# Two products of batch 0 by a second Strassen level, the softmax behind a later sum, and four small sums on GpSimd

## The chip, the cores and the metric

The kernel runs on one core of one Trainium2 chip. The metric is the device time of one execution in microseconds. The engines' names are those of the profile: PE is TensorE, DVE VectorE, ACT ScalarE, POOL GpSimd, and SP the queue that issues the transfers.

## The reference: what is computed

A cross attention between a sequence and a small state, and then a feed-forward layer over both results. All data is fp32.

```python
B, H, S, Ns, D = 8, 8, 512, 32, 64
scores = scale * x @ state^T                  # (B, H, S, Ns)
a = exp(scores - max); a /= a.sum(-1) + 1e-9
xread = a @ state                             # (B, H, S, D)
a2 = softmax of scale * state @ x^T           # the same scores, turned
sread = a2 @ x                                # (B, H, Ns, D)
x = concat(xread, sread) as 8 * 544 = 4352 rows of 512
h = x @ w_in                                  # 512 x 2048
g = where(h > 0, h, exp(min(h, 0)) - 1)
out = g @ w_out                               # 2048 x 512
```

The inputs are x (8, 8, 512, 64), state (8, 8, 32, 64), w_in (512, 2048) and w_out (2048, 512); the output has 4352 rows of 512.

## The kernel before

**Order.** No loop in the kernel runs as written. Every operation is recorded with a cost in a `Plan`; a list scheduler then brings all of them into one order, and each engine gets its instructions in that order. TensorE's operations are taken in the program's order as soon as they can start, the other engines' by a due time reckoned back from TensorE's; GpSimd's are kept in the order in which the program records them (L288), and transfers go through one queue, SP. `plan.behind(op)` (L189) makes all operations recorded under it, but those of GpSimd, wait for `op`. The profile puts all recorded operations at L466, the line of the helper that emits them, so they are told apart by their tiles.

**Batches.** The work goes batch by batch, 512 rows each. Batches 0 and 1 are computed together in `start()`, which also converts the weights into fp32 tiles and makes sums of them. Then come the rest of batch 1 (`ffn2_1`), batches 2 to 7 (`batch`, with `ffn2` as its second half), and the 256 rows of sread (`states`).

**The first layer of a batch.** The attention's weights are folded into the layer: `make_m` and `make_three` multiply the state with w_in (tile w_half, fetched from a DRAM copy, tile kT for the state) into tile m, and the softmaxed scores in aT are then multiplied with m. `ffn1_chunk` does this for a quarter of the 2048 columns by Strassen-Winograd with seven products: `sum_a` (L743) makes three sums of aT's blocks once per batch and `sum_m` four of m's for each quarter. `sum_a` runs on VectorE, `sum_m` on GpSimd. ELU goes through tile xe into tile g; batch 0's activations lie in `sec[:, :8192]` (called g0), all others' in g.

**Between two batches.** While the second layer of batch b runs on TensorE, `soft_next` (L1423) prepares batch b+1: `softmax` turns the scores by VectorE transposes into xr, takes maxima, subtracts them on GpSimd, takes exp on ScalarE, multiplies with the reciprocals on GpSimd, and transposes into aT; `softmax_rows` does the softmax along the other direction; `load_x` loads x into xe; `move_state` (L829) transposes xr and moves it by 16 transfers xr to xr; then `sum_a` and the first `sum_m`. All of it stands behind `late[3]`, the last of the sums of the second layer's product 4. `state_read` (L842) multiplies the moved xr with xe; ELU may overwrite xe only after it.

**The second layer.** g times w_out is a first level of Strassen-Winograd (class `Strassen`), seven products P1 to P7 of 256x256-blocks. A plain product (L1095) is 16 times two matmuls of 128x128 by 128x256 into one PSUM bank, and its result is then copied by ScalarE (`copy`) or added by VectorE (`plus`) into quarters of the output tile. In `ffn2` and `ffn2_1` most products go by a second level (class `Second`, L973): four sums of weights of 128x512 (`weights`, kept for all batches), three or four sums of activations (`sums`), and seven steps of four matmuls of 128x128 each (`steps`) in two banks x and y; after every step VectorE adds the bank into the output, and the next step in the same bank waits for it. The weights' sums of P7, P5, P4, P3 and P6 have homes of 1536 columns each in sec; `s_2` in sec holds two pairs of activation sums.

**Batch 0.** In `start()` batch 0's seven products are plain ones (object n0). In the order of the program: P1, P2, P6 (t_w[2]), P7 (t_w[3]), the scores of batch 2, P5 (t_w[1]), P4 (t_w[4]) and P3 (b22). `n1.sum_1()` between P5 and P4 makes batch 1's first sums. The weights' sums of 6, 7, 5, 4, 3 and 2 are all made in `ffn2_1`.

**Fetches.** Each batch fetches the halves 0 to 7 of w_in into three places of w_half, where half hc goes to place hc modulo 3; halves 5, 6 and 7 are recorded at the start of `batch` (L1523) for `make_three(b, (6, 7), 5)`.

Of the kernel before, what the change touches and what calls it, by code (L numbers as in the profile page):

```python
# [391 lines left out]
def kernel(  # L392
# [350 lines left out]
    def sum_a():  # L743

        r11, r12, r21, r22 = a_blocks_of(a_sb)
        t1, t2, t4 = (a_sb[:, 1024 + 256 * i : 1280 + 256 * i] for i in range(3))
        (V if 1 else Q).tensor_tensor(out=t1, in0=r12, in1=r11, op=ALU.subtract)
        (V if 1 else Q).tensor_tensor(out=t2, in0=r22, in1=t1, op=ALU.subtract)
        (V if 1 else Q).tensor_tensor(out=r12, in0=r22, in1=r12, op=ALU.subtract)
        (V if 1 else Q).tensor_tensor(out=t4, in0=r21, in1=t2, op=ALU.subtract)  # L750
# [168 lines left out]
    def ffn1_chunk(b, c, g_to):  # L919

        m = g_of[b, c]
        l11, l12, s3, l22 = m_blocks(m)
        s1, s2, s4 = (m[:, 1024 + 256 * i : 1280 + 256 * i] for i in range(3))
        r11, t3, r21, r22 = a_blocks_of(a_sb)
        t1, t2, t4 = (a_sb[:, 1024 + 256 * i : 1280 + 256 * i] for i in range(3))
        pa, pc, pb = bank(), bank(), fixed[c % 2].view()
        u2, u3 = (
            sec[:, 7680 + (c % 2 * 2 + i) * 512 : 7680 + (c % 2 * 2 + i + 1) * 512] for i in range(2)
        )
# [24 lines left out]
        return part_1, part_2  # L954
# [18 lines left out]
    class Second:  # L973

        def __init__(self, t, spare=None):
            self.t = t.rearrange("p (i k q) -> p i k q", i=3, q=P)
            self.spare = spare

        def blocks(self, b):
# [80 lines left out]
                steps.append(lambda args=args: step(*args))  # L1060
            return steps

    second = {
        k: Second(sec[:, i * 1536 : (i + 1) * 1536]) for i, k in enumerate((7, 5, 4, 3, 6))
    }
    second[2], second[1] = Second(sec_2), Second(sec_1)

    def spaces(ap, n=2):
        return [ap[:, i * 512 : (i + 1) * 512] for i in range(n)]

    s_2 = [spaces(sec[:, 7680 + i * 1024 : 7680 + (i + 1) * 1024]) for i in range(2)]

    class Strassen:

# [78 lines left out]
        for i in range(3)  # L1153
    ]

    def weight_block(n, parts=1):

        out = []
        for i in range(parts):
# [12 lines left out]
        return out  # L1172
# [16 lines left out]
    def start():  # L1189
# [23 lines left out]
        for what in 'swxtvyu':  # L1213
            if what == "s": load_states(0, 1, raw_s, q2)
            if what == "x": load_x(0, x_halves, q2)
            if what == "w": blocks[0] = weight_block(0, 2)
# [93 lines left out]
        y = o.open()  # L1310
        o.product(y, o.a21, t_w[3], True)
        o.copy(y, 1, 1)
        scores(2, xr, [f.view() for f in fixed] if 1 else None)
        softmax(2, a_sb)
        softmax_rows(2)
        load_x(2, x_halves)
        o.product(x1, o.s, t_w[1], False)
        o.plus(x1, 1, 1)
        n1.sum_1()
        o.product(y, o.a22, t_w[4], False)  # L1320
        o.plus(y, 1, 0)
        o.product(x1, o.a12, b22, False)
        o.copy(x1, 0, 1)
        for i in (1, 0):
            store(0, i, o)
        return n1, held[1]
# [30 lines left out]

    def ffn2(o, b):

        c11, c12, c21, c22 = (o.part(i, j) for i in range(2) for j in range(2))  # L1360
        nxt = b + 1 < B
        spare = spaces(m_sb[:, 1], 3)
        sl = 0
        if not sl: o.sum_1()
        late = [plan.ops[-1]]
        if 0:
# [55 lines left out]

        def soft_next():  # L1423
            if nxt:
                with plan.behind(late[3]):
                    softmax(b + 1, a_sb)
                    softmax_rows(b + 1)
                    load_x(b + 1, x_halves)
                    move_state(b + 1)
                    sum_a()  # L1430
                    if 1:
                        sum_m(m_to[0])
# [18 lines left out]
        for f in steps:  # L1451
            f()
        store(b, 0, o)

    def ffn2_1(o, b, x1):

# [30 lines left out]
        next_m(b + 1)  # L1487
# [34 lines left out]
    def batch(b):  # L1522
        for hc in range(5, 8) if 1 else range(4, 7):  # L1523
            fetch(hc)
        if b + 1 < B:
            load_blocks(b + 1, ob)
        else:
            make_ident()
# [105 lines left out]
    def states():  # L1634
# [7 lines left out]
        for hc in range(5):  # L1642
            fetch_state(hc)
        for k, i in second.items():
            if k > 1 or 0: i.restore()
# [102 lines left out]
```

## Time and profile before

| What | us |
|---|---|
| median of 4 runs | 696.54 |
| the runs | 695.88, 696.77, 696.47, 696.61 |
| the profiled execution's own time (the first of them) | 695.88 |
| its span, first to last instruction | 694.0 |
| TensorE busy (granted clock 1.000) | 684.4 |
| VectorE busy | 572.5 |
| ScalarE busy | 302.1 |
| GpSimd busy | 112.7 |

The span is 1.88 us shorter than the time; that part lies around the profiled instructions. A group or a timeline line gives engine, line, operation, the tile written and the tiles read, the shape and the number of instructions; in a timeline the first two numbers are the start and the length in us, and brackets give the idle time before and what ended it. A matmul of fp32 shows as two records, so x32 in a plain product is 16 matmuls, and x8 in a second-level step is four. Matmuls are pipelined, so their lengths overlap; the distance of two starts is the time that one takes.

### The profile page before, as it was taken

Reading aid. Unit: us, or ns where it says so; the run is one execution under the profiler, and the core shown is the slowest. Engines: PE = TensorE matmul, PEld = TensorE weight load, DVE = VectorE, ACT = ScalarE, POOL = GpSimd, SP = SyncE. Lnnn points to the kernel's source line nnn. Section 1 sums busy time; section 2 is a strip of 40 time slices with the busy share of each in tenths; the row PEclk is TensorE's granted clock in tenths of the full one; section 3 lists DMA queues with packets and bytes.
Section 4 is the critical chain, followed back from the end, with each engine's and each line's share of the span. In section 5 each row is a group of like instructions: output and inputs, shape, how many; then the busy total and the mean of one; then the engine's idle time right before and its main releaser. Section 6 shows DMA issues by size and latency. Waiting matters only on the chain.

```text
span 694.0 us, 14567 instructions
## 1 busy us (share of the span) xinstructions
PE 684.4 (99%) x5782; PEld 590.4 (85%) x5782; DVE 572.5 (82%) x1019; ACT 302.1 (44%) x640; POOL 112.7 (16%) x133
## 2 busy tenths in 40 slices
PE   8899999999999999999999999999999999999997
PEld 7444478889988998889988998899888998899996
DVE  5999999879949994999679985999499966997640
ACT  4999971003157313722275215731373227500530
POOL 0100000003330151104230243015110423000000
PEclk9999999999999999999999999999999999999999
DMA  9867873202281507450562218150745043200300
GB/s 234 259 203 253 278 240 51 61 31 92 80 218 38 122 20 231 87 122 4 177 156 81 44 47 243 46 123 19 240 78 123 2 150 126 61 1 32 122 8 24
DMA packets 111268, 78.55 MB, mean 113 GB/s; under 512 B 89184, under 2 KB 92768, under 8 KB 111200
## 3 DMA queue, kind: packets, MB, share of 16 engines
q1 hardware_dynamic: 108988, 77.06, 40.0%
q8 instruction: 46, 0.75, 0.5%
q10 hardware_dynamic: 2212, 0.56, 0.4%
q14 instruction: 22, 0.18, 0.1%
HBM read 61.34 MB, written 13.11 MB: 107 GB/s over the span
## 4 chain that ended last, share of the span: by engine, by line
PE 91%; ACT 3%; DMA 2%; SPq 1%; DVE 1%; issue 0%; ACTq 0%
PE ps L466 91%; SPq L466 1%; ACT sec L466 1%; DMA g<-in_x_dram 1%; DMA w_half<-w_in_mem 1%; ACT t_w L466 0%; DVE w_half L466 0%; ACT o L466 0%; DVE sec L466 0%; ACT w_half L466 0%; ACT m L466 0%; ACT g L466 0%; ACT s L466 0%; DVE t_w L466 0%; DVE g L466 0%
## 5 line engine op out<-in xcount | busy, mean ns | idle before, releaser
L466 PE MATMUL ps<-aT,m 128*128 128x256 f32 (+1 forms) x568 | 147.9, 405 | 0.1
L466 PE MATMUL ps<-w_out,g 128*128 128x128 f32 (+1 forms) x864 | 144.2, 314 | 0.0
L466 PEld LDWEIGHTS ps<-w_out,g 128*128 128x128 f32 x864 | 126.3, 191 | 12.4 <-issue 4.2
L466 PEld LDWEIGHTS ps<-aT,m 128*128 128x128 f32 x568 | 106.2, 190 | 29.4 <-issue 14.5
L466 DVE TENSOR_TENSOR o<-o,ps 128x128 f32<-128x128 f32 (+2 forms) x239 | 66.2, 281 | 41.3 <-PE ps L466 40.5
L466 ACT COPY o<-ps 128x128 f32<-128x128 f32 (+2 forms) x70 | 23.1, 335 | 147.4 <-PE ps L466 141.4
L466 POOL TENSOR_TENSOR xr<-xr,small 128x512 f32<-128x512 f32 x24 | 30.0, 1271 | 334.9 <-DVE small L466 171.1
L466 PE MATMUL ps<-sec 128*128 128x128 f32 x560 | 74.8, 277 | 0.0
L466 PEld LDWEIGHTS ps<-sec 128*128 128x128 f32 x560 | 68.5, 192 | 4.0 <-DVE o L466 3.7
L466 POOL TENSOR_TENSOR m<-m 128x256 f32<-128x256 f32 x72 | 60.5, 860 | 27.1 <-ACT m L466 25.7
L466 PE MATMUL ps<-t_w,s 128*128 128x128 f32 (+1 forms) x432 | 64.5, 298 | 0.0
L466 ACT ACTIVATE xe<-ps 128x512 f32<-128x512 f32 x96 | 54.9, 601 | 19.4 <-PE ps L466 12.8
L466 PEld LDWEIGHTS ps<-t_w,s 128*128 128x128 f32 x432 | 58.6, 192 | 2.5
L466 ACT COPY m<-ps 128x512 f32<-128x512 f32 (+1 forms) x56 | 28.1, 540 | 62.1 <-PE ps L466 55.7
L466 DVE SCALAR_TENSOR_TENSOR g<-xe,ps 128x512 f32<-128x512 f32 x66 | 43.7, 679 | 9.8 <-ACT xe L466 6.2
L466 DVE TENSOR_TENSOR ps<-sec,ps 128x512 f32<-128x512 f32 (+1 forms) x52 | 34.8, 669 | 13.9 <-ACT sec L466 7.0
L466 ACT COPY sec<-ps 128x512 f32<-128x512 f32 (+1 forms) x52 | 29.7, 571 | 28.6 <-PE ps L466 28.5
L466 PE MATMUL ps<-aT,s 128*128 128x256 f32 x168 | 41.2, 379 | 0.0
L466 ACT ACTIVATE xe<-xe 128x512 f32<-128x512 f32 x66 | 39.8, 636 | 0.7
L466 PEld LDWEIGHTS ps<-aT,s 128*128 128x128 f32 x168 | 31.9, 190 | 4.3
L466 PE MATMUL ps<-w_half,kT 64*32 64x256 f32 x1024 | 34.9, 381 | 0.5 <-DVE g L466 0.3
L466 PE MATMUL ps<-sec,g 128*128 128x128 f32 (+1 forms) x252 | 31.5, 272 | 1.2 <-DMA g<-in_x_dram 1.2
(149 smaller groups left out, 1108.6 us busy)
## 6 DMA issues: line engine op xcount, KB each, us to landing
w_half<-w_in_mem SPq DMA_DIRECT2D x54, 512.0 KB
t_w<-in_moe_w_out_dram SPq DMA_DIRECT2D x8, 1024.0 KB
t_w<-in_moe_w_in_dram SPq DMA_DIRECT2D x7, 1024.0 KB
out_dram<-o SPq DMA_DIRECT2D x14, 512.0 KB
xe<-in_x_dram SPq DMA_DIRECT2D x26, 256.0 KB
o<-in_x_dram SPq DMA_DIRECT2D x80, 64.0 KB
w_in_mem<-w_half SPq DMA_DIRECT2D x8, 512.0 KB
xr<-xr SPq DMA_DIRECT2D x96, 32.0 KB
```

The source lines that it names most:

```text
L466: ins = getattr(engine, name)(**named)
```

## The change

It does three things.

1. Batch 0's P4 and P3 go by the second level. For that, the weights' sums of 4 and 3 are made in `start()` and no longer in `ffn2_1`. The homes of the weights' sums of 4, 3, 7 and 5 and of `s_2` are rows of batch 0's own activations in sec (two by two, even rows for 4 and 3, odd rows for 7 and 5), and those of 6 stay behind them. P7's add into quarter (1, 0) is recorded right after P7, and P5's bank is copied into quarter (0, 1) right after its add into quarter (1, 1), because P4's and P3's steps are added to these quarters. The eight weights' sums of 4 and 3 and the activations' sums of both products run on VectorE in the time of batch 0.
2. What `soft_next` records stands behind `late[6]`, the last sum of activations of product 7, in place of `late[3]`, that of product 4; the sums of 6 and of 7 lie between.
3. `sum_a`'s four subtractions per batch go from VectorE to GpSimd.

TensorE's operations of `ffn2` also get the last `make_m` as something to wait for in the plan. Toggles that are off change nothing.

The program has 24 matmuls more on TensorE (56 in the place of 32), 24 operations more on GpSimd, two fewer on VectorE and as many as before on ScalarE and in the queue SP. In its order, the fetches of halves 5, 6 and 7 stand ahead of move_state's 16 transfers; before they stood behind them.

```diff
 def sum_a():
-        (V if 1 else Q).tensor_tensor(out=t1, in0=r12, in1=r11, op=ALU.subtract)
+        (V if 0 else Q).tensor_tensor(out=t1, in0=r12, in1=r11, op=ALU.subtract)
...
-    second = {
-        k: Second(sec[:, i * 1536 : (i + 1) * 1536]) for i, k in enumerate((7, 5, 4, 3, 6))
-    }
...
-    s_2 = [spaces(sec[:, 7680 + i * 1024 : 7680 + (i + 1) * 1024]) for i in range(2)]
+    if 1:
+        rows = sec[:, :8192].rearrange("p (r e c) -> p r e c", e=2, c=512)
+        homes = {
+            4: rows[:, 0:3, 0], 3: rows[:, 3:6, 0], 7: rows[:, 0:3, 1], 5: rows[:, 3:6, 1],
+            6: sec[:, 8192:9728],
+        }
+        second = {k: Second(homes[k]) for k in (7, 5, 4, 3, 6)}
+        s_2 = [[rows[:, 6, i], rows[:, 7, i]] for i in range(2)]
...
 in start():
         o.product(y, o.a21, t_w[3], True)
         o.copy(y, 1, 1)
+        if 1:
+            o.plus(y, 1, 0)
         scores(2, xr, [f.view() for f in fixed] if 1 else None)
         softmax(2, a_sb)
         softmax_rows(2)
         load_x(2, x_halves)
         o.product(x1, o.s, t_w[1], False)
         o.plus(x1, 1, 1)
-        n1.sum_1()
-        o.product(y, o.a22, t_w[4], False)
-        o.plus(y, 1, 0)
-        o.product(x1, o.a12, b22, False)
-        o.copy(x1, 0, 1)
+        if 1:
+            o.copy(x1, 0, 1)
+        if 1 < 2: n1.sum_1()
+        if 1:
+            second[4].weights(t_w[4])
+            second[4].sums(o.a22, s_2[0] + [sec_2[:, 1024:]])
+            steps = second[4].steps(o.part(1, 0))
+            second[3].weights(b22)
+            for f in steps:
+                f()
+            second[3].sums(o.a12, spaces(sec_2))
+            for f in second[3].steps(o.part(0, 1)):
+                f()
...
 in ffn2():
+        made = [op for op in plan.ops if op.name == "make_m"][-1]
+        first_op = len(plan.ops)
...
-                with plan.behind(late[3]):
+                with plan.behind(late[6]):
                     softmax(b + 1, a_sb)
                     softmax_rows(b + 1)
                     load_x(b + 1, x_halves)
                     move_state(b + 1)
                     sum_a()
...
+        for op in plan.ops[first_op:]:
+            if op.engine == PE and 1:
+                op.deps.add(made)
...
 in ffn2_1():
-        second[4].weights(t_w[4])
+        if not 1: second[4].weights(t_w[4])
...
-        second[3].weights(b22)
+        if not 1: second[3].weights(b22)
```

More of the change, by code (lines that the diff above doesn't have):

```diff
@@ L746, in sum_a @@
         t1, t2, t4 = (a_sb[:, 1024 + 256 * i : 1280 + 256 * i] for i in range(3))
-        (V if 1 else Q).tensor_tensor(out=t1, in0=r12, in1=r11, op=ALU.subtract)
-        (V if 1 else Q).tensor_tensor(out=t2, in0=r22, in1=t1, op=ALU.subtract)
-        (V if 1 else Q).tensor_tensor(out=r12, in0=r22, in1=r12, op=ALU.subtract)
-        (V if 1 else Q).tensor_tensor(out=t4, in0=r21, in1=t2, op=ALU.subtract)
+        (V if 0 else Q).tensor_tensor(out=t1, in0=r12, in1=r11, op=ALU.subtract)
+        (V if 0 else Q).tensor_tensor(out=t2, in0=r22, in1=t1, op=ALU.subtract)
+        (V if 0 else Q).tensor_tensor(out=r12, in0=r22, in1=r12, op=ALU.subtract)
+        (V if 0 else Q).tensor_tensor(out=t4, in0=r21, in1=t2, op=ALU.subtract)
     def a_blocks_of(a):
@@ L926, in ffn1_chunk @@
         pa, pc, pb = bank(), bank(), fixed[c % 2].view()
-        u2, u3 = (
-            sec[:, 7680 + (c % 2 * 2 + i) * 512 : 7680 + (c % 2 * 2 + i + 1) * 512] for i in range(2)
-        )
+        u2, u3 = s_2[c % 2]
         e = [xe[:, i * 512 : (i + 1) * 512] for i in range(4)]
@@ L975, in __init__ @@
         def __init__(self, t, spare=None):
-            self.t = t.rearrange("p (i k q) -> p i k q", i=3, q=P)
+            if len(t.shape) == 2:
+                t = t.rearrange("p (i c) -> p i c", i=3)
+            self.t = t.rearrange("p i (k q) -> p i k q", q=P)
             self.spare = spare
@@ L1061, in steps @@
             return steps
-    second = {
-        k: Second(sec[:, i * 1536 : (i + 1) * 1536]) for i, k in enumerate((7, 5, 4, 3, 6))
-    }
-    second[2], second[1] = Second(sec_2), Second(sec_1)
     def spaces(ap, n=2):
         return [ap[:, i * 512 : (i + 1) * 512] for i in range(n)]
-    s_2 = [spaces(sec[:, 7680 + i * 1024 : 7680 + (i + 1) * 1024]) for i in range(2)]
+    if 1:
[6 more added lines that the diff above has]
+        s_2 = [[rows[:, 6, i], rows[:, 7, i]] for i in range(2)]
+    else:
+        second = {
+            k: Second(sec[:, i * 1536 : (i + 1) * 1536]) for i, k in enumerate((7, 5, 4, 3, 6))
+        }
+        s_2 = [spaces(sec[:, 7680 + i * 1024 : 7680 + (i + 1) * 1024]) for i in range(2)]
+    second[2], second[1] = Second(sec_2), Second(sec_1)
     class Strassen:
@@ L1154, with weight_block @@
     ]
-    def weight_block(n, parts=1):
+    def weight_block(n, parts=1, only=None):
         out = []
-        for i in range(parts):
+        for i in range(parts) if only is None else (only,):
             k = 4 // parts
@@ L1215, in start @@
             if what == "x": load_x(0, x_halves, q2)
-            if what == "w": blocks[0] = weight_block(0, 2)
+            if what == "w": blocks[0] = weight_block(0, 2, 0 if "W" in 'swxtvyu' else None)
+            if what == "W": blocks[0] += weight_block(0, 2, 1)
             if what == "t": load_states(1, 2, raw_s[:, 1:], (SP,))
@@ L1318, in start @@
         o.plus(x1, 1, 1)
-        n1.sum_1()
-        o.product(y, o.a22, t_w[4], False)
-        o.plus(y, 1, 0)
-        o.product(x1, o.a12, b22, False)
-        o.copy(x1, 0, 1)
+        if 1:
[11 more added lines that the diff above has]
+                f()
+        else:
+            o.product(y, o.a22, t_w[4], False)
+            o.plus(y, 1, 0)
+            o.product(x1, o.a12, b22, False)
+            o.copy(x1, 0, 1)
+        if 1 == 2: n1.sum_1()
         for i in (1, 0):
@@ L1365, in ffn2 @@
         late = [plan.ops[-1]]
-        if 0:
+        if 0 or b in []:
             second[1].sums(o.a11, spare + s_2[0][:1])
@@ L1524, in batch @@
             fetch(hc)
+        if b in [][:1]: second[1].weights(b11)
         if b + 1 < B:
@@ L1644, in states @@
         for k, i in second.items():
-            if k > 1 or 0: i.restore()
+            if k > 1 or 0 or []: i.restore()
         xT = st["xT"].rearrange("p m b s -> p m (b s)")
```

## The prediction

> **What bounds the kernel now.** I read the page's first part and its chain, then the pieces of the chain in order of time, then the timelines of TensorE and VectorE around batch 0's products, and last all engines around one steady boundary between batches (300 to 350 us).
>
> The page: busy time, chain by engine, two GpSimd groups.
>
> ```profile
> PE 684.4 (99%) x5782; PEld 590.4 (85%) x5782; DVE 572.5 (82%) x1019; ACT 302.1 (44%) x640; POOL 112.7 (16%) x133
> PE 91%; ACT 3%; DMA 2%; SPq 1%; DVE 1%; issue 0%; ACTq 0%
> L466 POOL TENSOR_TENSOR xr<-xr,small 128x512 f32<-128x512 f32 x24 | 30.0, 1271 | 334.9 <-DVE small L466 171.1
> L466 POOL TENSOR_TENSOR m<-m 128x256 f32<-128x256 f32 x72 | 60.5, 860 | 27.1 <-ACT m L466 25.7
> ```
>
> The chain in order of time (start, us, what), its end.
>
> ```profile
> 62.20 427.89 PE ps L466 x3561
> 490.09 7.42 DMA w_half<-w_in_mem
> 497.51 0.04 issue
> 497.55 191.77 PE ps L466 x1536
> ```
>
> TensorE is the bound from 62.20 on: one chain without a gap, but for the third fetch of a weight half at 497.55. So a matmul saved after 62 us is time saved, and a wait of TensorE is time lost; what the other engines do counts only where TensorE stands behind it.
>
> TensorE (start, length), batch 0's products and four later second-level steps.
>
> ```profile
> 135.03 7.07 PE L466 MATMUL ps<-t_w,s 128*128 128x256 f32 x32
> 141.94 7.07 PE L466 MATMUL ps<-t_w,sec 128*128 128x256 f32 x32
> 148.85 7.07 PE L466 MATMUL ps<-w_out,sec 128*128 128x256 f32 x32
> 155.75 1.95 PE L466 MATMUL ps<-t_w,s 128*128 128x128 f32 x16
> ...
> 166.22 1.06 PE L466 MATMUL ps<-t_w,s 128*128 128x128 f32 x8
> ...
> 169.80 0.39 PE L466 MATMUL ps<-sec,g 128*128 128x128 f32 x2
> ```
>
> The starts are what to read: P5 at 135.03, P4 at 141.94, P3 at 148.85, the next work at 155.75. P4 and P3 last 6.91 and 6.90 us. Four steps of four matmuls run from 166.22 to 169.80, 0.895 us each.
>
> VectorE in the same place.
>
> ```profile
> 130.42 1.17 DVE L466 TENSOR_TENSOR s<-s,sec 128x1024 f32<-128x1024 f32 x1
> 131.52 0.67 DVE L466 TENSOR_TENSOR sec<-w_out 128x512 f32<-128x512 f32 x1
> ...
> 138.69 1.23 DVE L466 TENSOR_TENSOR s<-g 128x1024 f32<-128x1024 f32 x1 [2.76 <-PE ps L466]
> ```
>
> It has no pause up to 135.9, and then waits 2.76 us for TensorE. A 512-wide sum starts 0.60 us after the one before it, a 1024-wide one 1.13, a 128x128 add 0.20.
>
> The steady boundary.
>
> ```profile
> 313.56 2.05 POOL L466 TENSOR_TENSOR xr<-xr,small 128x512 f32<-128x512 f32 x2 [32.98 <-PE ps L466]
> 322.11 3.04 POOL L466 TENSOR_TENSOR xr<-xr,small 128x512 f32<-128x512 f32 x2 [6.50 <-DVE small L466]
> 322.41 1.82 DVE L466 TENSOR_TENSOR s<-s,g 128x1024 f32<-128x1024 f32 x1
> 327.85 10.07 SPq L466 DMA_DIRECT2D xr<-xr  x16
> 337.05 1.89 PE L466 MATMUL ps<-aT,m 128*128 128x256 f32 x8
> 341.55 1.10 PE L466 MATMUL ps<-xe,xr 128*32 128x64 f32 x64
> ```
>
> **The change, part by part.**
>
> (a) *TensorE's work.* P4 and P3 were 13.81 us. They become 14 steps: 14 x 0.895 = 12.53. Term: -1.28 us.
>
> (b) *What the steps wait for.* The weights' sums of 4 and 3 (eight 512-wide sums) and both products' activation sums move onto VectorE at batch 0, where it was already full up to 135.9. In the built program its queue runs as before up to the second s<-s,sec (three sums in, four out, so 0.60 earlier: ends 130.9). Then 11 sums of 0.60: 137.5. P7's add, 0.60: 138.1. Four more sums: 140.5. Then in order s<-g (1.13), a sum (0.60), g<-g,s (1.13), P5's add into quarter (1,1) (0.60), s<-g (1.13), the add of P4's step 0 (0.20), g<-g,s (1.13), the add of step 1 (0.20). Their ends: 141.7, 142.3, 143.4, 144.0, 145.1, 145.35, 146.5, 146.7.
> On TensorE, P5 ends at 141.94, steps 0 and 1 at 143.73, and then the scores of batch 2 stand. They alternate between two banks, and one of them held P5. That bank is first added by VectorE (144.0) and then copied by ScalarE into quarter (0,1); the built program makes the copy wait for the add. With 0.4 for the copy (the mean of ScalarE's copies into o is 335 ns) and two handovers of about 0.15 (VectorE's idle between a matmul's end and its add at 322.20), the scores get the bank at about 144.75 instead of 143.73, a stall of 1.0 us. Step 2 wants step 0's add (145.35) and finds it done; step 3 wants step 1's add (146.7) and starts about 0.2 us late. Behind step 3 I followed the queue to 161 us and found no further wait above 0.1. Term: +1.2 us. Bounds: 0 (VectorE some 1.3 us further than I reckon) and +1.3 (all of the lateness of step 1's add). I take 1.2, since the queue is told by rows of this very place.
> What hides the remaining VectorE work (eight sums, 4.8 us, twelve net adds of 0.2) is that batch 1's steps lose the same eight sums; they ran without a wait of TensorE before, so that gain is nothing.
>
> (c) *The third fetch.* Before, fetches 5, 6, 7 are issued at 338.02, behind the 16 transfers of move_state, and the matmuls that need them start at 346.30; at the one boundary of the chain they landed 7.42 us after issue and TensorE stood some 0.4 us. In the new SP order they stand ahead of move_state, right behind the matmuls that free their slots (which end at 330.7), so some 15 us before their use. Term: -0.4, between 0 and -0.8 (twice the one seen).
>
> (d) *The softmax, two sums later.* Its transposes xr<-ps now wait for the sums of 7, in the profile the g<-g sum that ends at 317.97; with 3.7 us of softmax work out of its way (two transposes at 0.63, four reductions at 0.60) that sum ends by some 314.9 and the transposes start near 315.5, against 308.21. From there to the first aT transpose was 16.1 us; I take 17.3 to 18.5, since the reductions now lie between more adds. So aT is ready at 332.8 and 334.4. Behind it:
> - GpSimd: the four sums of aT at 0.84 each (the 3.35 of four m<-m at 325.10), 334 to 337.1, then the m<-m to 340.4. POOL keeps program order, so these m<-m wait behind them. TensorE's first aT pair in the new order needs none of the sums; five steps lie behind it, and the sums are first needed about 342.3. Slack 2 to 4 us. VectorE loses four sums of 0.33 to 0.42.
> - SP: move_state issues from about 335.85 (xr<-xr transposes 8 us later than 326.41) for 10.07 us (11.98 at the longest of the boundaries), last packets 1.0 us behind the last issue: 346.9 to 348.8. The transfers now share the queue with the three fetches. State_read in the new order stands behind 14 aT matmuls (0.43 each), five steps and make_three (1.45): 337.05 + 11.97 = 349.0. Slack 0.2 to 2.1 us. Behind state_read stand all matmuls of the next batch, and ELU, which overwrites xe.
> - VectorE beside GpSimd: the pair of GpSimd operations took 2.05 alone and 3.04 where s<-s,g ran, and that took 1.82 instead of 1.22; under m<-m at 331.58 the 512-wide sums took 0.84, 0.87 and 1.21 instead of 0.68. Four new GpSimd sums per batch meet VectorE sums before P3's steps, whose adds (due about 337.9) stand behind them: 0 to 0.2 us per boundary.
> GpSimd's sums of aT come at six boundaries (batches 2 to 7), the later softmax at five (3 to 7). Term for all: +0.3. Lower end 0: TensorE has no wait here that could go. Upper end +4, if state_read comes 0.8 late at each of five.
>
> A rule that speaks against this part: the Trainium skill's "SBUF — State Buffer", section "Who interferes with whom", says that a VectorE instruction with two SBUF inputs and a GpSimd one that reads SBUF exclude each other for the whole instruction. Read so, each of 24 sums could hold VectorE for its full 0.84, and if one in two fell ahead of an add that TensorE wants, the sum would be 10 us worse (an estimate). The rows above show 0.16 to 0.6 of lengthening per sum, not a full block, and adds that read PSUM stay at 0.28 to 0.29 under the same GpSimd work; I go by the rows.
>
> Sum against the profiled execution (span 694.0, its time 695.88, the lowest of four): 695.88 - 1.28 + 1.2 - 0.4 + 0.3 = 695.7. The median, 696.54, lies 0.66 above it, for reasons no view shows; a change that takes a fetch's lateness away may take some of that too. I predict 695.8.
>
> **The rivals.**
> - *VectorE is in time* (faster). P4's stall in (b) is 0: 695.88 - 1.28 - 0.4 + 0.2 = 694.4. For it: VectorE idles 2.76 us before 138.69 today and my lateness is only about 1 us, a sixth of what I summed. Against: the bank of P5 goes through two engines before the scores.
> - *State_read comes late* (slower). move_state's last transfers land behind 349.0. At 0.6 us for each of five boundaries: 695.7 - 0.3 + 3.0 = 698.4. It decides from a softmax about 1 us later than I reckon, or transfers that take over 12 us behind the fetches; above 0.5 us per boundary the kernel is slower in measure (695.7 - 0.3 + 2.5 = 697.9). For it: the slack is the smallest of all here, and every piece of the chain before it crosses three engines. Against: 1 us of middle slack.
> - *The fetches stay late* (no part of (c) comes): 696.1, inside the forecast.
>
> **How the numbers follow.** 0.2% of 696.54 is 1.39 us, about what a measurement can tell from no change: faster is below 695.15, slower above 697.93. The forecast (part of the gain eaten, 695.2 to 697.0) has 0.43, with the late fetches in it; VectorE in time 0.32; state_read late 0.25. Faster 0.33, same 0.43, slower 0.24, as little of each case spills over. The range goes from 694.3 (the faster case, less its last tenth) to 698.6 (state_read 0.64 late).
>
> **What would show it.** (a) 14 steps 0.895 us apart where P4 and P3 were. (b) A gap of about 1 us before or within the scores near 144, with VectorE's add of P5 at 143.4 to 144; right if it is there, wrong if the steps run on. (c) No DMA piece near 497 in the chain. (d) POOL's aT sums ending by 338, state_read near 349 with no gap before it; a gap there, five times, is the slower rival. I am wrong altogether if TensorE shows new waits in batch 1's steps or between aT matmuls.

## The result and the profile after

The changed kernel is 2 us slower.

| | before | after |
|---|---|---|
| median, us | 696.72 (71 runs) | 698.71 (44 runs) |
| lowest and highest, us | 695.35, 700.26 | 696.28, 701.95 |
| ratio, 95% interval | | 1.0026 (1.0019 to 1.0033) |
| profiled execution: its time, its span, us | 695.88, 694.0 | 697.24, 695.4 |

Two numbers have to be explained, and they are not the same: the two profiled executions differ by 1.36 us, the medians by 1.99. The forecast was 695.8, with a range up to 698.6.

The page of the changed kernel, busy time by engine; and the end of the chain of waits (start, length, what).

```profile
PE 686.0 (99%) x5830; PEld 591.2 (85%) x5830; DVE 564.7 (81%) x1017; ACT 302.7 (44%) x640; POOL 123.1 (18%) x157
```

```profile
62.75 121.52 PE ps L466 x817
184.27 0.03 issue
184.30 166.16 PE ps L466 x1522
350.46 0.06 issue
350.52 340.21 PE ps L466 x2926
```

The chain still runs on TensorE alone from 62 us on, and the piece that waited for the third fetch is gone. But such a chain hides short waits inside its pieces; they show only where the distance of two starts is longer than the work. Laying the two traces side by side, from the start of the TensorE-bound stretch (62.20, now 62.75) to its end (689.32, now 690.73) the difference of 1.41 us falls into three parts:

- +0.55 before that stretch begins. This is start-up (loads and weight conversion); in the other profiles of this study the stretch begins anywhere from 62.0 to 63.6, but for one whose start was put in another order (67.39).
- -0.02 from P5 to the scores of batch 3 (135.03 to 226.04 before, 135.58 to 226.57 after). The second level's 1.28 us are gone again by then.
- +0.88 at the five steady boundaries. Their periods were 75.21, 75.21, 75.21, 75.62 (0.41 of it the fetch) and 74.32, and are 75.45, 75.60, 75.42, 75.42 and 74.56.

TensorE around batch 0's scores, after (start, length).

```profile
141.63 1.03 PE L466 MATMUL ps<-t_w,s 128*128 128x256 f32 x4
142.49 1.95 PE L466 MATMUL ps<-t_w,sec 128*128 128x128 f32 x16
144.37 1.86 PE L466 MATMUL ps<-xr,kT 64*32 64x512 f32 x16
146.16 1.16 PE L466 MATMUL ps<-sec 128*128 128x128 f32 x8
```

VectorE in the same place.

```profile
140.92 1.21 DVE L466 TENSOR_TENSOR s<-g 128x1024 f32<-128x1024 f32 x1
142.06 0.68 DVE L466 TENSOR_TENSOR sec<-t_w,sec 128x512 f32<-128x512 f32 x1
142.66 1.21 DVE L466 TENSOR_TENSOR g<-g,s 128x1024 f32<-128x1024 f32 x1
143.79 0.68 DVE L466 TENSOR_TENSOR m<-m,ps 128x512 f32<-128x512 f32 x1
```

The scores (the row with 64x512) take 1.79 us from their start to the next step; undisturbed they take 1.02. So TensorE waits 0.77 us there, and about 0.2 more behind it. The last VectorE row is the add of P5's bank that the scores stand behind; it starts at 143.79, and VectorE has no pause ahead of it from 117 us on. In the profile of before VectorE stood idle 2.76 (ahead of 138.69), 0.44, 0.30 and 2.76 us in this stretch:

```profile
142.21 0.69 DVE L466 TENSOR_TENSOR m<-m,ps 128x512 f32<-128x512 f32 x1 [0.44 <-PE ps L466]
145.59 0.69 DVE L466 TENSOR_TENSOR t_w<-t_w 128x512 f32<-128x512 f32 x1 [0.30 <-PE ps L466]
149.05 0.69 DVE L466 TENSOR_TENSOR m<-m,ps 128x512 f32<-128x512 f32 x1 [2.76 <-PE ps L466]
```

One steady boundary after: GpSimd, the transfer queue and TensorE.

```profile
332.43 2.05 POOL L466 TENSOR_TENSOR xr<-xr,small 128x512 f32<-128x512 f32 x2 [10.26 <-DVE small L466]
334.45 0.72 POOL L466 TENSOR_TENSOR aT<-aT 128x256 f32<-128x256 f32 x1
335.56 2.10 POOL L466 TENSOR_TENSOR aT<-aT 128x256 f32<-128x256 f32 x3 [0.39 <-DVE aT L466]
```

```profile
331.67 1.29 SPq L466 DMA_DIRECT2D w_half<-w_in_mem  x3
336.83 10.08 SPq L466 DMA_DIRECT2D xr<-xr  x16
```

```profile
347.36 2.86 PE L466 MATMUL ps<-aT,m 128*128 128x256 f32 x12
350.15 1.42 PE L466 MATMUL ps<-xe,xr 128*32 128x64 f32 x64
351.50 1.78 PE L466 MATMUL ps<-aT,m 128*128 128x256 f32 x7
```

The three fetches now go 5 us ahead of move_state's 16 transfers, which have all landed at 347.86. State_read (the row with xe,xr) starts at 350.15 directly behind the matmuls ahead of it: no wait for data. It now stands between matmuls of aT, and from its start to that of the next matmul it takes 1.35 us. Before it took 1.03, from 341.55 to 342.58:

```profile
341.55 1.10 PE L466 MATMUL ps<-xe,xr 128*32 128x64 f32 x64
342.58 1.16 PE L466 MATMUL ps<-sec,g 128*128 128x128 f32 x8
```

At the five boundaries it now takes 1.19, 1.35, 1.16, 1.16 and 1.20 us, 0.9 more in all than five times 1.03.

### The profile page after: what moved, and what is told of

Read it like the earlier page. It is cut to its first block, busy times and chain, and to the rows that moved or that the text cites. A ratio compares the mean times of both kernels' runs of the same rounds, so it can differ in the third digit from the quotient of the medians.

```text
span 695.4 us, 14665 instructions
## 1 busy us (share of the span) xinstructions
PE 686.0 (99%) x5830; PEld 591.2 (85%) x5830; DVE 564.7 (81%) x1017; ACT 302.7 (44%) x640; POOL 123.1 (18%) x157
## 4 chain that ended last, share of the span: by engine, by line
PE 92%; ACT 3%; SPq 1%; DMA 1%; DVE 1%; issue 0%; ACTq 0%
PE ps L466 92%; SPq L466 1%; ACT sec L466 1%; DMA g<-in_x_dram 1%; ACT t_w L466 0%; DVE w_half L466 0%; ACT o L466 0%; DVE sec L466 0%; ACT w_half L466 0%; ACT m L466 0%; ACT g L466 0%; ACT s L466 0%; DVE t_w L466 0%; DVE g L466 0%; ACT kT L466 0%
## 5 line engine op out<-in xcount | busy, mean ns | idle before, releaser
L466 POOL TENSOR_TENSOR xr<-xr,small 128x512 f32<-128x512 f32 x24 | 25.4, 1077 | 380.7 <-DVE small L466 223.8
L466 PE MATMUL ps<-sec 128*128 128x128 f32 x592 | 78.8, 276 | 0.0
L466 PEld LDWEIGHTS ps<-sec 128*128 128x128 f32 x592 | 72.0, 192 | 1.9 <-DVE o L466 1.0
L466 POOL TENSOR_TENSOR m<-m 128x256 f32<-128x256 f32 x72 | 58.3, 831 | 16.1 <-ACT m L466 13.9
L466 DVE TENSOR_SCALAR xe<-xe 128x512 f32<-128x512 f32 x30 | 15.4, 529 | 45.9 <-ACT xe L466 45.7
```

Source lines behind the costliest of these rows:

```text
L466: ins = getattr(engine, name)(**named)
```

## The experiments

Theory: the new work fills VectorE's pauses in batch 0, so that VectorE's lateness there, whatever its cause, now reaches TensorE. Rivals: the boundaries' +0.88 is the whole loss, and the second level is as good as free; or VectorE has room and only its order is at fault. Each time stands beside executions of the kernel before, measured along with it on the same chip, and "+" is the difference of the two medians in us.

### The kernel again, and without the second level in batch 0

The changed kernel unaltered.

> The changed kernel once more, for its spread and a second profile. In the first profile the steady boundary is 0.2 to 0.4 us longer than before, at state_read, which now stands among aT matmuls, without waiting for its transfers (they had landed 2 us earlier). Theory 'order' (the cost is the place of state_read in TensorE's order): the same gaps again, median 698.5 +- 0.6. Theory 'late' (in the slower executions state_read or the aT matmuls wait for move_state or the sums of aT): a slower execution shows waits of 0.3 to 1 us per boundary there. Theory 'clock': slower executions show a granted clock of 0.996 to 0.997 and no new gap.

The same with P4 and P3 as plain products and their weights' sums back in `ffn2_1`; the softmax behind late[6] and the sums of aT on GpSimd stay.

```diff
-    if 1:
+    if 0:
         rows = sec[:, :8192].rearrange("p (r e c) -> p r e c", e=2, c=512)
...
-        if 1:
+        if 0:
             second[4].weights(t_w[4])
...
-        if not 1: second[4].weights(t_w[4])
+        if not 0: second[4].weights(t_w[4])
...
```

> P4 and P3 of batch 0 as plain products again, the homes of the weights' sums as before; the softmax behind late[6] and the sums on GpSimd stay. By the two profiles the second level there saves 1.3 us of matmuls and costs 1.0 us at the scores and 0.2 at the steps behind, net -0.1: 698.6 to 699.0 here. If the second level of P4 and P3 is what made the kernel slower: 696.5 to 697.5.

Measured: 698.63 for the changed kernel (11 runs, +2.05, ratio 1.0029, 1.0018 to 1.0040), 696.94 with P4 and P3 plain (11 runs, +0.36, ratio 1.0011, 1.0002 to 1.002). So with the second level of P4 and P3, which takes 1.28 us of matmuls off TensorE, the kernel is 1.7 us slower than without it; the rest of the change costs some 0.4.

The two profiles show why, because both happened to meet the same disturbance. ScalarE's timeline (brackets: idle before, and what ended it), first of the unaltered kernel, then with P4 and P3 plain:

```profile
70.85 1.14 ACT L466 ACTIVATE w_out<-t_w 128x1024 f32<-128x1024 f32 x1 [1.56 <-DMA t_w<-in_moe_w_out_dram]
```

```profile
70.55 1.14 ACT L466 ACTIVATE w_out<-t_w 128x1024 f32<-128x1024 f32 x1 [1.59 <-DMA t_w<-in_moe_w_out_dram]
```

A block of w_out came 1.6 us late from DRAM; its transfer was issued no later than in the changed kernel's profile above (61.78 and 61.83 us). In that profile there is no such wait (this instruction starts at 69.12), nor in that of before (68.81). The wait is there in 8 of the 17 profiles of this case, 0.72 to 1.64 us long, in kernels with and without the second level. What follows from it differs. The unaltered kernel, TensorE and then the chain:

```profile
144.31 1.04 PE L466 MATMUL ps<-xr,kT 64*32 64x512 f32 x2
146.73 1.09 PE L466 MATMUL ps<-xr,kT 64*32 64x512 f32 x14 [1.37 <-ACT m L466]
147.74 1.16 PE L466 MATMUL ps<-sec 128*128 128x128 f32 x8
```

```profile
145.46 0.61 DVE m L466
146.07 0.02 issue
146.09 0.59 ACT m L466
146.68 0.04 issue
146.73 39.13 PE ps L466 x406
```

With P4 and P3 plain, VectorE and then the chain:

```profile
138.83 1.23 DVE L466 TENSOR_TENSOR s<-g 128x1024 f32<-128x1024 f32 x1 [1.25 <-PE ps L466]
...
142.35 0.69 DVE L466 TENSOR_TENSOR m<-m,ps 128x512 f32<-128x512 f32 x1 [0.44 <-PE ps L466]
...
149.19 0.69 DVE L466 TENSOR_TENSOR m<-m,ps 128x512 f32<-128x512 f32 x1 [2.76 <-PE ps L466]
```

```profile
62.34 627.84 PE ps L466 x5217
```

With plain products the first of VectorE's pauses shrinks from 2.76 to 1.25 us, the next two are 0.44 and 2.76 as before, and TensorE runs on unbroken. With the second level there is no pause to shrink: P5's add comes at 145.38 in place of 143.79, and the scores last 147.74 - 144.31 = 3.43 us in place of 1.79. VectorE's 1.59 us have become 1.64 us of TensorE. From P5's start to the scores of batch 3 TensorE takes 91.01 us before and 90.99 after with the block in time; with the block late it takes 91.01 with plain products (135.18 to 226.19) and 92.62 in the unaltered kernel (135.53 to 228.15). VectorE's idle time in batch 0 was not spare: it took up the scatter of the loads.

### More and less work for VectorE, in the order of the changed kernel

A list scheduler answers most edits with another order (below). So for these three the finished order was kept, and only VectorE's load changed in it (`dve` lists VectorE's operations in that order). First, the last s<-g sum ahead of P5's add is made three times, which is 2.27 us more; once in the changed kernel, and once with P4 and P3 plain, where the same sum is dve[168].

```diff
+    dve = [op for op in steps if op.engine == DVE]
...
+        if op is dve[176]:
+            for _ in range(2):
+                op.emit()
```

> The changed kernel in its own order, with the first s<-g sum of batch 1 (1024 wide, 1.13 us) made three times in a row, 2.27 us more for VectorE ahead of the add of P5. Theory 'VectorE's queue': all of it reaches TensorE, 700.6 to 701.1. If VectorE is not what bounds this place: less than 0.5 us more.

> P4 and P3 plain (as in a4) with the same sum made three times. VectorE idles 2.76 us for TensorE just ahead of it and 2.8 us before P4's add, so theory 'VectorE's queue' expects most of the 2.27 us to be hidden: 696.9 to 697.5, against 696.9 without. If extra VectorE work costs its time here as well, 699.2.

Measured: 703.19 in the changed kernel (6 runs, +6.4, that is 4.4 more than unaltered), 697.92 with P4 and P3 plain (12 runs, +1.15, 0.8 more than without the extra sums). Both lie above the theory's ranges, 700.6 to 701.1 and 696.9 to 697.5. In the profile with plain products, whose block was 1.64 us late, the extra work cost nothing in batch 0: VectorE still has pauses of 1.19 and 1.16 us, and from P5 to the scores of batch 3 TensorE takes 91.01 us as before; where the median's 0.8 lies is open. In the changed kernel the same stretch takes 93.51 us in place of 90.99, so there all of the 2.27 is passed on, as the theory has it. But 4.4 is about twice that. The profiled execution, 699.43, is the lowest of the six and 2.2 us above the unaltered kernel's profiled one. VectorE and TensorE in it:

```profile
140.49 3.75 DVE L466 TENSOR_TENSOR s<-g 128x1024 f32<-128x1024 f32 x3
...
145.90 0.68 DVE L466 TENSOR_TENSOR m<-m,ps 128x512 f32<-128x512 f32 x1
```

```profile
143.96 1.04 PE L466 MATMUL ps<-xr,kT 64*32 64x512 f32 x2
147.25 1.09 PE L466 MATMUL ps<-xr,kT 64*32 64x512 f32 x14 [2.25 <-ACT m L466]
```

Its block of w_out was in time and its mean granted clock 0.998; the other five have 702.96 to 704.31 at mean clocks of 0.994 to 0.996. The profile of the next kernel shows what such a mean can come from. Here the eight weights' sums of 4 and 3 are made by GpSimd in place of VectorE, at the same places of the order.

```diff
+            self.ops = list(zip(
+                plan.ops[first:], [t1, t2, t4, self.b12],
...
+    for k in (4, 3):
+        for op, o, i, j in second[k].ops:
+            op.emit = issue(
+                nc.gpsimd, "tensor_tensor", dict(out=o, in0=i, in1=j, op=ALU.subtract)
+            )
```

> The changed kernel in its own order, with only this different: the eight weights' sums of products 4 and 3 run on GpSimd, which is idle from 62 to 147 us, so VectorE is relieved of 4.8 us (less what two engines reading the same memory take from each other) before the add of P5. Everything else keeps its place in the order. Theory 'VectorE's queue': the wait at batch 0's scores goes, in slower executions too, 695.7 to 697.0 in place of 698.6, and the spread narrows. If the 2 us lie in the clock or at the boundaries: 698.6.

Measured: 703.76 (6 runs, +7.0). GpSimd and VectorE:

```profile
133.42 2.24 POOL L466 TENSOR_TENSOR t_w<-t_w 128x512 f32<-128x512 f32 x1
```

```profile
132.25 2.29 DVE L466 TENSOR_TENSOR s<-s,sec 128x1024 f32<-128x1024 f32 x1
134.46 1.75 DVE L466 TENSOR_TENSOR sec<-sec 128x512 f32<-128x512 f32 x1
...
141.16 0.68 DVE L466 TENSOR_TENSOR m<-m,ps 128x512 f32<-128x512 f32 x1
```

The two engines hold each other up: VectorE's sums of two SBUF tiles take 1.75 and 2.29 us in place of 0.68 and 1.21, the add that reads PSUM stays at 0.68. Five of VectorE's 512-wide sums end 0.55 us behind the GpSimd sum that ran beside them, so VectorE waited for that sum's end. VectorE got later, not earlier (P5's add at 147.99), and TensorE stood longer. Windows of the same profile: us, then PE, PEld, DVE, ACT, POOL busy with their counts, the granted clock, DMA share, GB/s.

```profile
147.00:148.10 1.10, 0.00 (x0) 0.00 (x0) 1.10 (x2) 0.00 (x0) 0.00 (x0) 1.00 0.00 0
148.10:148.50 0.40, 0.00 (x0) 0.00 (x0) 0.40 (x1) 0.00 (x0) 0.00 (x0) 0.60 0.00 0
148.50:154.90 6.40, 5.56 (x31) 3.90 (x32) 5.03 (x9) 0.59 (x1) 0.00 (x0) 0.50 0.01 3
154.90:155.20 0.30, 0.30 (x4) 0.30 (x4) 0.16 (x1) 0.00 (x0) 0.25 (x1) 0.81 0.00 0
```

TensorE's records end at 145.37 and go on at 149.34. At about 148.2 the granted clock falls to a half, and it comes back at about 155.0, 6.8 us later, of which TensorE works for 5.7: some 2.8 us lost on top of the wait. Such a fall takes 0.005 off the mean clock of the execution. Four of the five longer executions of the tripled sum have such a mean, 0.994, so the second half of their 4.4 us is put down to a fall like this one; none of them was profiled. In the profile of the tripled sum the gap of 2.25 us left the clock at 1.00.

The Trainium skill's "TensorE: Matmul & The Clock Gate" (Part 1) has the clock go to half after an idle window of about 3.4 us, and says that this window runs freely. The gaps of 3.97 and 2.25 us agree with the first. But the length of a gap does not decide alone: in the profile of the softmax put back behind late[3] (below) the clock was at a half for 3.4 us, from 518.4, after a gap of only 1.56 us. TensorE's row, then a window as above:

```profile
517.69 1.37 PE L466 MATMUL ps<-w_out,g 128*128 128x256 f32 x4 [1.56 <-DVE g L466]
```

```profile
518.50:521.70 3.20, 3.20 (x9) 2.57 (x8) 1.88 (x3) 0.57 (x1) 3.20 (x4) 0.50 0.65 92
```

A window of free phase would explain why executions of one kernel fall on both sides; no run here tests it.

This touches the changed kernel itself. Of its 45 executions (the 44 and the profiled one), 12 have a mean granted clock of 0.996 or 0.997, and those are 12 of its 13 longest, 699.87 to 701.95; the others have 0.998 to 1.000. Of the 11 further executions above, the two longest, 700.25 and 700.39, have 0.997 and 0.996; of 95 executions of the kernel before that stand beside the experiments, two have 0.996. That is 0.002 to 0.003 below most, half of what a fall of 6.8 us takes; a fall of 3.4 us would fit, and cost up to 1.7 us. With the block late, the gap in TensorE's records at the scores is 1.37 us, near those 1.56, but in that profile the clock stayed at 1.00. That these executions are ones in which the clock fell at the scores is argued, not shown: none of them was profiled. As an estimate from these numbers, 1.63 us (92.62 - 90.99) in 8 of 17 executions and 1.7 in 12 of 45 make 1.2 us in the mean; the unaltered kernel's mean lies 1.5 above that with plain products (698.70 and 697.21).

### P5's add moved ahead

If VectorE's order were the fault, an order in which P5's add and the first steps' adds go ahead of sums that are needed later should give the 1.28 us back. Five VectorE instructions were moved back in the finished order.

```diff
+    for a, b in [(197, 198), (182, 204), (184, 185), (178, 183), (180, 178)]:
+        steps.remove(dve[a])
+        at = steps.index(dve[b]) + 1
...
+        steps.insert(at, dve[a])
```

> The changed kernel in its own order, with five VectorE instructions of batch 0 moved behind more pressing ones: the second half of a g<-g,s sum and one s<-g sum stand behind the add of P5 and the adds of P4's first two steps, another g<-g,s sum 20 instructions later, one transpose and one sum behind an add. No work is added or taken. Theory 'VectorE's queue and then the clock': P5's add comes 1.13 us earlier, the wait at the scores is shorter by that in every execution, and fewer executions wait long enough for the granted clock to fall: 697.2 to 697.9 in place of 698.6, with fewer executions at 0.997 and below. If the order on VectorE does not matter: 698.6.

Measured: 698.67 (12 runs, +1.6, ratio 1.0023, 1.0012 to 1.0033), between 697.70 and 699.78, with clocks of 0.998 to 1.000 throughout. TensorE:

```profile
144.13 1.09 PE L466 MATMUL ps<-xr,kT 64*32 64x512 f32 x16
...
157.13 1.16 PE L466 MATMUL ps<-w_out,sec 128*128 128x128 f32 x8 [0.37 <-DVE m L466]
...
164.27 1.16 PE L466 MATMUL ps<-sec,s 128*128 128x128 f32 x8 [0.29 <-DVE o L466]
```

The wait at the scores is gone, in a profile whose block was in time, and with it the longest executions; but the waits come back 13 and 20 us later, and from P5 to the scores of batch 3 this profile takes 91.98 us, 0.99 more than the changed kernel's. This order gives nothing back: VectorE is without a pause from 144.2 to 176.7 us, and where it is late only moves. That no other order does better is not shown.

### One product at a time

P4 alone by the second level; P3 alone; and P4 alone without the other two parts of the change (late[3], `sum_a` on VectorE).

```diff
-        if 1:
-            o.copy(x1, 0, 1)
         if 1 < 2: n1.sum_1()
-        if 1:
-            second[4].weights(t_w[4])
...
+        second[4].weights(t_w[4])
+        second[4].sums(o.a22, s_2[0] + [sec_2[:, 1024:]])
+        for f in second[4].steps(o.part(1, 0)):
+            f()
+        o.product(x1, o.a12, b22, False)
+        o.copy(x1, 0, 1)
...
-        if not 1: second[3].weights(b22)
+        if not 0: second[3].weights(b22)
```

> The changed kernel with only P4 by the second level and P3 plain (its weights' sums back in batch 1); the softmax behind late[6] and the sums on GpSimd stay. VectorE then gets about 6 us more in batch 0 (four weights' sums and four activation sums at 0.60, seven adds at 0.20) in place of about 12; in the kernel before it idled some 6 us there (2.76 + 0.44 + 0.30 + 2.76). Theory 'VectorE is full': this much fits, so the 0.64 us of matmuls saved come through: 696.2 to 696.9, against 696.9 with both plain and 698.6 with both by the second level. If half the work costs half: 697.8.

> The same with only P3 by the second level and P4 plain. Same theory: 696.2 to 696.9. If what matters is the handover of P5's bank to the scores (P5's add, then ScalarE's copy, which this kernel keeps, P4's does not): 697.5 to 698.

> Only P4 by the second level, and nothing else of the change: the softmax behind late[3], sum_a on VectorE. TensorE's and the queue's orders at the steady boundary are those of the kernel before. Theory 'VectorE is full': 695.8 to 696.4, a little faster than the kernel before, if no wait comes back in batch 1. If any second-level product in batch 0 costs: 697.5.

Measured, 12 runs each: 698.22 (+1.4, ratio 1.0017, 1.0005 to 1.0029), 697.69 (+0.9, 1.0016, 1.0002 to 1.0030) and 697.58 (+0.8, 1.0013, 1.0002 to 1.0025). So the theory that half the work fits (696.2 to 696.9, and 695.8 to 696.4) missed in all three. Against +0.36 with both plain, P4 costs 1.1 and P3 0.55; their sum is about the 1.7 of both, but each interval is some 0.8 us wide to either side. The third kernel differs from the first by parts 2 and 3 of the change alone, which the medians put at 0.6 us. Half the load is no version that wins. P4 alone has VectorE again without a pause up to P5's add at 143.91, since the scheduler pulled other sums forward into the free place. P3 alone leaves VectorE pauses of 1.77 and 1.04 us, has no wait at the scores, so the handover of P5's bank is not what it costs, but one of about 0.5 at 174.3.

### The parts of the change apart

The softmax back behind late[3]; `sum_a` back on VectorE; both back, so that the second level of P4 and P3 stands alone.

```diff
-                with plan.behind(late[6]):
+                with plan.behind(late[3]):
```

```diff
-        (V if 0 else Q).tensor_tensor(out=t1, in0=r12, in1=r11, op=ALU.subtract)
+        (V if 1 else Q).tensor_tensor(out=t1, in0=r12, in1=r11, op=ALU.subtract)
...
```

> The softmax behind the sums of product 4 again (late[3]); the other two parts stay. State_read stands between second-level steps again and the transfers of move_state are issued about 8 us earlier. Theories 'order' and 'late': 1.2 to 2 us less than the changed kernel, 696.7 to 697.5; under 'late' the spread narrows too. If the cost sits in batch 0 or in GpSimd's sums: no change from 698.7. The fetches of 5, 6 and 7 stand behind move_state again: up to 0.4 us more.

> sum_a on VectorE again; the other two parts stay. State_read stays among aT matmuls. Theory 'order': no change, 698.7 +- 0.5. If GpSimd's sums of aT hold VectorE or come late: 1 us less or more. Theory 'late': between, since aT's sums no longer stand in front of the sums of m.

> Only the second level of P4 and P3, as the change has it; the softmax behind late[3] and sum_a on VectorE as before. Theory 'VectorE's queue': a wait of 1 to 3 us at the scores against 1.28 us saved: 696.6 to 698.4, with the wide spread of the changed kernel. If the spread comes from the boundary: 696.5 with the spread of before.

Measured: 708.06 (4 runs, +11.5), 707.01 (4 runs, +10.4) and 699.85 (6 runs, +3.0, ratio 1.0042, 1.0025 to 1.0058). The first two missed their expectations by 10 us: each half of the boundary's change, taken without the other, leads the scheduler to another order in every batch. In the first, make_three moves behind some 24 matmuls of aT, and what needs it stands:

```profile
361.66 1.97 PE L466 MATMUL ps<-w_out,g 128*128 128x256 f32 x8 [1.09 <-DVE g L466]
```

They tell nothing of the cost of either part, only that under this scheduler the two parts belong together. The third lies 1.5 above its range; it waits 0.74 us at the scores, 0.2 behind them and about 0.4 at 175, and has boundaries of up to 76.17 us; the second level without the others is no better than with them.

Batch 1's first sums behind P5's add, once in the changed kernel and once with the old boundary:

```diff
-        if 1 < 2: n1.sum_1()
+        with plan.behind([op for op in plan.ops if op.engine == DVE][-1]):
+            n1.sum_1()
```

> The changed kernel with batch 1's first sums (n1.sum_1, four 1024-wide, 4.5 us of VectorE) held behind the add of P5 in batch 0, so VectorE has some 2 us in hand when P5 ends instead of being 1.3 us late. Theory 'VectorE's queue' (batch 0's scores and steps wait for a VectorE that is late, and every lateness of the weights' loads passes through to TensorE): the wait at the scores goes, 696.8 to 697.3 in place of 698.6, and the spread narrows. If the clock or the boundary set the 2 us: no change, 698.6.

> The same, and the softmax behind late[3] and sum_a on VectorE as before: only the second level of P4 and P3 is left of the change, with VectorE relieved. Theory 'VectorE's queue': the matmuls saved (1.28 us) come through: 695.3 +- 0.5, faster than both kernels. Theory 'matmuls of 128 columns gain nothing here': 696.6.

Measured: 699.04 (5 runs, +2.2) and 705.09 (6 runs, +8.2). In the first VectorE stands idle 3.26 us before P5's add and the scores run on at 144.36 without a wait, as the theory has it, but batch 1 was put in another order and waits at 178 to 210 us; the second has the same, more of it, and its clock at a half for about 6.8 us from 210.3. Neither time tells what the second level costs with VectorE relieved.

Last, the kernel before with state_read placed among aT's matmuls, as the change has it:

```diff
+        st["sr"] = plan.ops[-1]
...
+            if c == 0 and b > 2:
+                st["sr"].deps.add(plan.ops[-1])
```

> The kernel before, with state_read of batches 3 to 7 held until three aT pairs have run, so it stands among aT matmuls as in the changed kernel; its data is there long before. Theory 'order': each boundary is 0.2 to 0.3 us longer with no wait, 1.0 to 1.5 us in all: 697.6 to 698.1, less any third-fetch wait. If the place of state_read costs nothing: 696.6.

Measured: 703.92 (4 runs, +7.0). In its profile some 7 us lie before batch 0's P5, where the start was put in another order: P5 begins at 143.12 in place of 135.03, now behind the scores. The boundaries can be read: 75.31, 75.30 and, at the last, 74.38 against 75.21, 75.21 and 74.32; the two between, 75.80 and 75.48, are longer, one of them by a wait for a transfer. So the place of state_read accounts for some 0.1 of the 0.2 us or more that a boundary became longer. State_read itself takes 1.03 us here at all five, as before: the 1.16 to 1.35 of the changed kernel does not come from its neighbours alone.

## Why the prediction was wrong

**What held.** (a) The second-level steps came 0.9 us apart, as reckoned. (b) in the profiled execution came at its place and nearly in its size: P5's add was forecast to run from 143.4 to 144.0 and started at 143.79, on a TensorE that is 0.55 later from its start on; the stall at the scores was forecast at 1.0 and is 0.77, with 0.2 behind it, as forecast. (c) The chain has no DMA piece any more. Of (d) the times held: the sums of aT end at 337.66 (forecast by 338), move_state issues at 336.83 (335.85, and TensorE by then runs 0.8 behind the prediction's clock), state_read starts at 350.15 without a wait. So the second rival did not happen, though its time, 698.4, is close to the measured one: the kernel is slower for another reason.

**The step that failed: the bounds of (b).** "Bounds: 0 [...] and +1.3 (all of the lateness of step 1's add)". That lateness was summed from the rows of one execution, in which the loads had come in time, and treated as a constant. It is not: in 8 of 17 profiles a block of w_out comes 0.72 to 1.64 us late, and in the one of the unaltered kernel VectorE reaches P5's add 1.59 us later. Before the change, pauses of 6 us in all took that up. The change fills them with sixteen sums and fourteen net adds (the prediction counted twelve), some 12 us of VectorE work, and from then on the lateness passes to TensorE: the wait at the scores is 0.77 us in one profile and 2.4 in the other. The upper bound had to be about 1.2 + 1.6 = 2.8, and more where the wait is long enough for the clock to fall. The prediction had the fact in hand, and used it wrongly: it named VectorE's idle 2.76 us as an argument for the faster rival, not as cover that the change uses up. In the two profiles with the block in time (a) + (b) came to -0.02, close to the -0.1 forecast; in the two with the block late to +1.61. In medians the second level costs +1.7.

**The term that was mis-sized: (d).** +0.3 for all boundaries; the profiles show +1.29 before the 0.41 of (c) is taken off. The prediction looked for a wait and there is none; the boundary is longer at state_read: 0.1 per boundary goes with its new place, and 0.13 to 0.32 lie inside it (1.16 to 1.35 us in place of 1.03), for a reason that no row shows. In medians, parts 2 and 3 with (c) cost +0.36 (interval of the ratio 1.0002 to 1.002) with P4 and P3 plain and 0.6 with P4 by the second level, where (c) + (d) gave -0.1.

**The anchor.** The sum was made against the lowest of four runs, and the 0.66 up to the median were "for reasons no view shows". VectorE's pauses, which a view showed, would have told how much lateness of the loads the kernel can bear. The gap from the profiled execution to the median grew from 0.84 (696.72 - 695.88) to 1.47 us (698.71 - 697.24).

**The rule on the shared port.** The prediction went by rows that showed 0.16 to 0.6 us of lengthening, against the Trainium skill's "SBUF — State Buffer" ("Who interferes with whom"), by which the port pair that the two engines share is an exclusive lock, and a VectorE instruction with two SBUF inputs contends for it with a GpSimd one that reads SBUF. With GpSimd and VectorE side by side on sums of 128x512, VectorE's sum took 1.75 us for 0.68 and GpSimd's up to 2.24: here the rule is right. The prediction's own row is no case against it: the first GpSimd operation of the pair at 322.11 ends at 323.15, the s<-s,g sum that started at 322.41 ends 1.08 us after that (it takes 1.22 alone), and the second GpSimd operation takes 2.03 us for 1.05. That is the same lock, with less overlap. For the aT sums of the change it did not decide the sum: no TensorE wait at the boundary came of it.

**What stays open.** Why the block of w_out comes late in about half of the profiles; whether it is the clock that makes the changed kernel's twelve long executions, and where it falls in them; and why state_read itself takes longer in the changed kernel. No version of this study is faster than the kernel before.

## What to carry to other kernels

Before an idle engine is filled, read what its idle time absorbs: subtract the new work from the pauses, and price the lateness that no longer fits at its worst, not at what one profile had. A profile is one execution; where its time is the lowest of the runs shown, the others hold delays that it doesn't show, and the sum needs a term for them. Under a list scheduler, part of a change can cost five times the whole through another order, so a single cost is measured in a frozen order.

## What the hardware showed that was not expected

- The clock: after a gap of 3.97 us in TensorE's records the granted clock was 0.50 for 6.8 us (148.2 to 155.0), and again for about 6.8 us where two waits of 1.44 and 0.96 us stood close together (from 210.3, batch 1's first sums moved with the old boundary). After a gap of 2.25 us it stayed at 1.00, but in the kernel with the softmax back behind late[3] it was 0.50 for 3.4 us (518.4 to 521.8) after a gap of 1.56 us. So the length of one gap did not tell whether the clock fell.
- GpSimd as a helper: eight 128x512 sums moved from VectorE to GpSimd made VectorE later, P5's add at 147.99 in place of 143.79, as VectorE's sums of two SBUF tiles waited for the GpSimd sum beside them (1.75 us in place of 0.68) and GpSimd's took 1.49 to 2.24 us.
